# Clustered attention and a gated FFT layer on one core: engine order written by hand, dependent steps put off by a set number of places, reciprocal rows spread by two DMAs

## The chip, the cores and the metric

One core of a Trainium2 chip. The metric is the device time of one execution in microseconds (us), lower is better. The engines are PE (matmul; its weight loads are shown as PEld), DVE (vector), ACT (scalar activation), POOL (GpSimd) and SP, which here issues DMAs only. Each engine takes its own instructions in order and waits at semaphores for the others; sixteen DMA engines move data.

## The reference

The first half is attention in which a query only sees keys of its own cluster; the second half is a long convolution by FFT between two gates.

```python
B, H, S, D = 4, 8, 768, 64          # n_clusters = 16
q_assign = argmax(einsum('bhsd,hcd->bhsc', q_n, c_n))      # q_n, k_n, c_n: normalised
k_assign = argmax(einsum('bhsd,hcd->bhsc', k_n, c_n))
mask = q_assign[:, :, :, None] == k_assign[:, :, None, :]
scores = where(mask, q @ k.T / sqrt(D), -1e9)
attn = softmax(scores)
x = (attn @ v).transpose(0, 2, 1, 3).reshape(B, S, H * D)  # (4, 768, 512)
x1, x2, x3 = split(x @ w_proj, 3)                          # w_proj: 512 x 1536
x2_conv = irfft(rfft(x2, axis=1) * rfft(filter_fft, axis=0))
out = (x1 * x2_conv * x3) @ w_out                          # (4, 768, 512)
```

Inputs and output are float32 in HBM.

## The kernel before

The work runs in eight groups (`groups`): one batch and four of its eight heads. A group has two pairs of heads (`Pair`), a pair has six steps, one for each block of 128 keys. That makes 96 steps; w is the step within the group (0 to 11), sk the step within the pair (0 to 5).

**A step.** For each of the two heads, `scores` (L332) multiplies keys by queries into a PSUM tile ps (two buffers), and ACT takes the exponential into one of six SBUF tiles p (L336). The cluster mask is part of the matmul: `routing` writes the one-hot cluster of each row, times a large number, into extra rows of the operand aug. Scores of step i + 1 are issued ahead of the `values` of step i. `values` (L347) multiplies the p of both heads by v into the PSUM tile o (one buffer), and DVE adds p up over the six steps in acc (L354, from sk = 1 on; acc has one buffer). After sk = 5 ACT copies o to osb (L357, L358).

**Finish of a pair.** In step sk = 0 of the next pair `finish` (L372) runs. PE sums acc over the 128 partitions with a matrix of ones (L366), ACT copies the four rows of sums to den (L369). The reciprocals are needed spread over partitions, and that is done through DRAM: den to dd (L376), dd to dn as 128 x 12 (L378), DVE adds a small number and inverts dn (L379, L380), dn to dr (L382), and one DMA copies the two rows of dr to 64 partitions each of rb (L384; 384 KB, its source has the shape 2 x 64 x 768 with a repeated middle dimension). All four DMAs are issued by SP. DVE then scales osb by rb into x32 (L387), and `store` writes the sums and differences uT on DVE (L419, L420) and xT on POOL (L421). The last pair of all takes another way, over PE (`finish_on_pe`).

**Fill places.** Between a step's matmuls stand fills: the generators `routing` (of the next group), `hyena` (the second half of the model, for the batch before) and `tables` (in group 0). Each `yield` ends one fill. A list `fill` holds a generator, the number of fills it has left and the step by which it should be through; from these each step works out its number nf and issues half of them after the scores of the first head and half after those of the second (`emit`). One fill of PE work ends in a PSUM tile pf (two buffers) that ACT or DVE reads.

`routing` transposes q and k (L271, copies on ACT L273, casts into aug on POOL L278 and L279) and has SP load the next q and k into the buffer just read (L86); matches with the centroids (L284), transposes the result (L293), and finds the first best cluster on DVE (L295, L296, then L300, L302, L304, which give the one-hot oh). After three empty fills PE transposes oh (L310), DVE writes ohT (L312), and SP copies it to aug with eight DMAs (L316). `hyena` projects (L436), multiplies by the spectrum of the filter (`convolve`: L249 and L253 on PE, L447 on DVE, L450 on POOL), computes gates (L460, L463, L465), transforms back (`invert`: L478, a copy od on ACT L481, yy on DVE L485 and L486, y2 on POOL L487) and projects out (L499). `tables` loads the filter (L200, L201), forms its sum and difference on DVE (L217, L218) and its spectrum. `forward_tables` makes the sine tables: arithmetic on DVE (L185 to L190), the sines on ACT (L192).

**Order.** `tc.manual_schedule` is given PE alone (L529): PE's instructions keep the order in which the program issues them. Those of ACT, DVE, POOL and SP, DMA issues among them, are put in order by the scheduler of the framework before the run, by its own estimate of when operands are ready, so they may be moved ahead of instructions that the program issues earlier.

Of the kernel before, what the change touches and what calls it, by code (L numbers as in the profile page):

```python
# [13 lines left out]
F32 = mybir.dt.float32  # L14
# [3 lines left out]
Alu = mybir.AluOpType  # L18
# [12 lines left out]
def kernel(  # L31
# [11 lines left out]
    nc = tc.nc  # L43
    ctx.enter_context(nc.allow_non_contiguous_dma(reason="layouts"))
    B, H, S, D = q.shape
# [8 lines left out]
    EPS = 1e-30  # L54
# [11 lines left out]
    def bank():  # L66
        if spare:
            return spare.pop(0)
        if more_banks[0]:
            more_banks[0] += 1  # L70
            if more_banks[0] % 4 in (0, 2):
                w = psS.tile([128, 2, 512], F32, name="ps")
                spare.append(w[:, 1])
                return w[:, 0]
        return psF.tile([128, 512], F32, name="pf")[:]


    raw = ctx.enter_context(tc.tile_pool(name="raw", bufs=4))
# [28 lines left out]
    c = cen.tile([128, D], F32)  # L107
# [50 lines left out]
    at = ctx.enter_context(tc.tile_pool(name="at", bufs=1))  # L158
# [19 lines left out]
    nc.gpsimd.memset(kc[:, 0, 192:193], 384.0)  # L178
    nc.gpsimd.memset(sh[:, 0, 192:193], 192.0)

    def forward_tables():
        MAGIC = 12582912.0
        for m in range(3):
            sm = cen.tile([128, 1], F32)
            nc.vector.tensor_scalar(sm, sq, float(2 * m), None, op0=Alu.add)  # L185
            n, r = (pbuf[2 * m + i][:, :S].rearrange("p (a b) -> p a b", a=2) for i in range(2))
            nc.vector.scalar_tensor_tensor(n, kc, sm, sh, op0=Alu.mult, op1=Alu.add)
            nc.vector.tensor_scalar(r, n, 1.0 / S, MAGIC, op0=Alu.mult, op1=Alu.add)
            nc.vector.tensor_scalar(r, r, MAGIC, -float(S), op0=Alu.subtract, op1=Alu.mult)
            nc.vector.tensor_tensor(n, n, r, op=Alu.add)  # L190
            for i in range(2):
                nc.scalar.activation(fw[i][:, m], n[:, i], Act.Sin, scale=2.0 * math.pi / S)  # L192

# [66 lines left out]
    def routing(n):  # L260
        aset, g = n % NSET, n % 2
        qkT = {}
        for pr in range(2):
            for j in range(2):
                qr = qk_raws.pop((n, pr, j))
                z = 2 * pr + j
                qkT[z] = rt.tile([128, 2, 384], F32, name="qkT", bufs=4)
                for ch in range(2):
                    tps = bank()
                    for t in range(3):  # L270
                        nc.tensor.transpose(tps[:, ts(t, 128)],  # L271
                                            qr[:, 3 * ch + t].rearrange("p h d -> p (h d)"), ident)
                    nc.scalar.copy(qkT[z][:, ch], tps[:, :384])  # L273
                    if ch == 1:
                        load_qk(n + 1, pr, j)
                    yield
                qf = qkT[z][:].rearrange("p a b -> p (a b)")
                (nc.gpsimd if n else nc.vector).tensor_copy(augs[aset][0][:D, z], qf[:D])  # L278
                nc.gpsimd.tensor_copy(augs[aset][1][D:, z], qf[D:])  # L279
        sim = rt.tile([128, 2, 384], F32, name="sim")  # L280
        for ch in range(2):
            sim_ps = bank()
# [19 lines left out]
        nc.vector.tensor_reduce(m2, cf, axis=AX, op=Alu.max)  # L302
        oh = rt.tile([128, 48, NC], BF16, name="oh")
        nc.vector.tensor_tensor(oh, cf, m2[:].unsqueeze(2).to_broadcast([128, 48, NC]), op=Alu.is_equal)  # L304
        for _ in range(3):
            yield
        ohf = oh[:].rearrange("p n c -> p (n c)")
        oT = bank()[:].bitcast(BF16)
# [12 lines left out]
    class Pair:  # L321
# [17 lines left out]
        def values(self, sk):  # L339
# [13 lines left out]
                    a = pb[hp][0][:, :S] if sk == 1 else acc[hp]  # L353
                    nc.vector.tensor_tensor(acc[hp], a, pb[hp][sk][:, :S], op=Alu.add)  # L354
            if sk == NT - 1:
                self.osb = at.tile([128, S + 1], F32, name="osb", bufs=2)
                nc.scalar.copy(self.osb[:, :384], self.o[:, 0, :384])  # L357
                nc.scalar.copy(self.osb[:, 384:], self.o[:, 1, :385])  # L358

        def sums(self):  # L360

# [10 lines left out]
        def finish(self):  # L372

            den = self.sums()
            dd = dram.tile([4, 384], F32, name="dd")
            nc.sync.dma_start(dd, den[0:128:32])  # L376
            dn = at.tile([128, 12], F32, name="dn")
            nc.sync.dma_start(dn, dd[:].rearrange("z (a b) -> (z a) b", b=12))  # L378
            nc.vector.tensor_scalar(dn, dn, EPS * S, None, op0=Alu.add)  # L379
            nc.vector.reciprocal(dn, dn)  # L380
            dr = dram.tile([2, S], F32, name="dr")
            nc.sync.dma_start(dr[:].rearrange("z (a b) -> (z a) b", b=12), dn)  # L382
            rb = at.tile([128, S], F32, name="rb")
            nc.sync.dma_start(rb, dr[:].unsqueeze(1).to_broadcast([2, 64, S]))  # L384
            x32 = at.tile([128, NT, 128], F32, name="x32")
            xf = x32[:].rearrange("p t c -> p (t c)")
            nc.vector.scalar_tensor_tensor(xf, self.osb[:, :S], self.osb[:, S:S + 1], rb,  # L387
                                           op0=Alu.add, op1=Alu.mult)
            self.store(x32)

        def finish_on_pe(self):

# [31 lines left out]
    def hyena(b, xT, uT, last=False):  # L424
# [16 lines left out]
        def convolve():  # L441
            for i in range(3):
                tm = [hw.tile([128, 2, DM], F32, name="tm", bufs=3) for r in range(2)]
                for cs in range(2):
                    ps = spectrum(i, cs, uv2[:, 0], uv2[:, 1])
                    for r in range(2):
                        nc.vector.tensor_tensor(tm[r][:, cs], ps, hm[:, i, 2 * r + cs], op=Alu.mult)  # L447
                    yield
                for r in range(2):
                    (nc.vector if last and r else nc.gpsimd).tensor_tensor(  # L450
                        y[:, i, r], tm[r][:, 0], tm[r][:, 1], op=Alu.add)

        def gates(dt):
            x3 = pbuf[dt][:, :S] if last else hw.tile([128, S], F32, name="x3", bufs=2)
# [13 lines left out]
        def invert(dt):  # L468
            po, pe = bank(), bank()
            steps = [(0, 0, 0, 0, 128), (0, 1, 1, 0, 128), (2, 0, 4, 0, 64), (2, 1, 5, 0, 64)]  # L470
            for n in range(4):
# [7 lines left out]
                                     start=(n == 0), stop=(n == 3))  # L479
            od = hw.tile([128, 384], F32, name="od")  # L480
            nc.scalar.copy(od, po[:, :384])  # L481
            yy = hw.tile([128, NT, 128], F32, name="yy")
            ov = od[:].rearrange("p (t c) -> p t c", c=64)
            ev = pe[:, :384].rearrange("p (t c) -> p t c", c=64)
# [1 line left out]
            nc.vector.tensor_tensor(yy[:, :, 64:], ev, ov, op=Alu.subtract)  # L486
            (nc.vector if last and dt % 2 else nc.gpsimd).tensor_tensor(  # L487
                y2[:, dt], yy[:].rearrange("p t c -> p (t c)"), gate[dt], op=Alu.mult)
            yield
            yield  # L490

        def expand():
# [32 lines left out]
        for _ in gen:  # L525
            pass

    NR, NH, NTAB = 17, 43, 13
    ctx.enter_context(tc.manual_schedule(engines={mybir.EngineType.PE}))  # L529
    groups = [(b, g) for b in range(B) for g in range(2)]  # L530
    more_banks[0] = 1
    drain(routing(0))
    more_banks[0] = 0
    forward_tables()
    nc.gpsimd.memset(augs[1][1][:D], 0.0)
    load_v(*groups[1])
    xu = {}
# [17 lines left out]
    def emit(nf):  # L555
        for _ in range(nf):
            for f in fill:
                if f[1] > 0:
                    f[1] -= 1
                    next(f[0], None)  # L560
                    break
# [4 lines left out]
    for i, (n, pr, sk) in enumerate(steps):  # L566
# [15 lines left out]
        if w == 4 and n == 0:  # L582
            nc.gpsimd.dma_start(wpj, moe_w_proj.rearrange("(t p) m -> p t m", p=128))
            nc.gpsimd.dma_start(wout, moe_w_out.rearrange("(t p) m -> p t m", p=128))
        if w == 5 and g == 0 and n > 0:
            hq = hyena(b - 1, *xu[b - 1])
            fill.append([hq, NH // 2, 12])

        nf = 0
        for f in fill:  # L590
            nf += -(-f[1] // max(1, f[2] - w))
        scores(i + 1, 0)
        emit((nf + 1) // 2)
        scores(i + 1, 1)
        emit(nf // 2)
        if sk == 0 and i:
            pairs[steps[i - 1][:2]].finish()
        pairs[n, pr].values(sk)
    fin = pairs[steps[-1][:2]].finish_on_pe()
    for _ in range(4):  # L600
        next(fin, None)
# [34 lines left out]
```

## Time and profile before

| | us |
|---|---|
| median of 2 runs (650.2 to 653.59) | 651.89 |
| the profiled execution, its own time | 651.56 |
| its span, first to last instruction | 649.7 |
| PE busy | 455.3 (70%) |
| DVE busy | 341.5 (53%) |
| ACT busy | 259.3 (40%) |
| POOL busy | 151.4 (23%) |
| mean granted PE clock, as a share of 2.4 GHz | 0.865 |

The profile is of one execution. Busy time leaves out semaphore waits, branches and the issuing of DMAs. An instruction's idle time is put down to the one that released it last. The granted clock has two levels here, 1.0 (2.4 GHz) and 0.5 (1.2 GHz). "SPq" rows are DMA issues on SP: the time on the row is that of the issue, not of the transfer.

### The profile page before, as it was taken

The numbers are of one execution on the slowest core, as the hardware profiler recorded it, in microseconds if no ns is written. First come the engines' busy times: TensorE is split into PE (matmuls) and PEld (weight loads), VectorE is DVE, ScalarE is ACT, GpSimd is POOL, SyncE is SP. The second block draws the span as 40 slices with busy tenths as digits, with TensorE's granted clock in tenths as the row PEclk, the third lists the DMA queues.
The fourth block names the chain that finished last, engine by engine and source line by source line (L and its number), as shares of the span: only waits on it lengthen the run. The fifth ranks groups of instructions, "written<-read, shape, count | busy, mean of one in ns | idle before, by whom it ended". The sixth has DMA issues, their size and how long they took to land.

```text
span 649.7 us, 6805 instructions
## 1 busy us (share of the span) xinstructions
PE 455.3 (70%) x2426; PEld 184.8 (28%) x2426; DVE 341.5 (53%) x474; ACT 259.3 (40%) x430; POOL 151.4 (23%) x154
## 2 busy tenths in 40 slices
PE   1538899089249587779785885789667688958565
PEld 0323334034113242224222342323222233313221
DVE  0937655572836535453652835553553755832632
ACT  2434576147214262337353262436334146324021
POOL 6500514101403241222300541222300430210211
PEclk9959899689759697799999798889879699779798
DMA  9930423104300042005410041004000000002002
GB/s 255 202 74 7 96 68 90 49 14 113 72 23 11 17 113 59 13 14 168 97 30 25 1 126 47 12 24 150 22 17 21 5 2 26 1 25 97 0 1 97
DMA packets 66518, 37.05 MB, mean 57 GB/s; under 512 B 56042, under 2 KB 61734, under 8 KB 66486
## 3 DMA queue, kind: packets, MB, share of 16 engines
q1 hardware_dynamic: 61430, 32.14, 17.7%
q0 software_dynamic: 1088, 2.13, 1.7%
q10 hardware_dynamic: 3968, 2.36, 1.5%
q8 instruction: 19, 0.31, 0.2%
q14 instruction: 13, 0.11, 0.0%
HBM read 30.66 MB, written 6.48 MB: 57 GB/s over the span
## 4 chain that ended last, share of the span: by engine, by line
PE 42%; DMA 23%; DVE 19%; issue 6%; ACT 6%; POOL 1%; SPq 1%; DVEq 0%; ACTq 0%; POOLq 0%
DMA rb<-dr 19%; PE o L347 15%; PE ps L332 7%; PE pf L460 5%; PE pf L499 3%; DMA dr<-dn 2%; PE pf L366 2%; PE pf L478 2%; DVE tm L447 2%; DMA vraw<-in_v_dram 1%; PE ps L460 1%; PE pf L436 1%; POOL hy L487 1%; DVE uT L420 1%; ACT qkT L273 1%
## 5 line engine op out<-in xcount | busy, mean ns | idle before, releaser
L347 PE MATMUL o<-p_141,vraw 128*64 128x385 f32 (+1 forms) x128 | 58.1, 584 | 0.0
L347 PE MATMUL o<-p_142,vraw 128*64 128x385 f32 (+1 forms) x128 | 58.1, 584 | 0.0
L336 ACT ACTIVATE p_144<-ps 128x768 f32<-128x768 f32 x32 | 26.3, 822 | 76.7 <-PE ps L332 75.9
L460 PE MATMUL pf<-xT,wpj 128*128 128x384 bf16 x212 | 46.4, 351 | 9.8 <-DVE tm L447 6.6
L347 PE MATMUL o<-p_146,vraw 128*64 128x385 f32 (+1 forms) x128 | 52.1, 533 | 0.0
L347 PE MATMUL o<-p_145,vraw 128*64 128x385 f32 (+1 forms) x128 | 52.1, 533 | 0.0
L310 PE MATMUL pf<-identb,oh 128*128 128x128 bf16 x42 | 5.1, 283 | 64.8 <-DVE oh L304 64.8
L347 PE MATMUL o<-p_144,vraw 128*64 128x385 f32 (+1 forms) x128 | 48.9, 506 | 0.0
L347 PE MATMUL o<-p_143,vraw 128*64 128x385 f32 (+1 forms) x128 | 48.9, 505 | 0.0
L336 ACT ACTIVATE p_145<-ps 128x768 f32<-128x768 f32 x32 | 25.9, 810 | 54.9 <-PE ps L332 54.9
L336 ACT ACTIVATE p_141<-ps 128x768 f32<-128x768 f32 x32 | 25.9, 811 | 41.9 <-PE ps L332 37.1
L450 POOL TENSOR_TENSOR hy<-tm 128x512 bf16<-128x512 f32 x21 | 28.1, 1353 | 51.1 <-DVE tm L447 31.7
L336 ACT ACTIVATE p_142<-ps 128x768 f32<-128x768 f32 x32 | 26.1, 815 | 29.6 <-PE ps L332 27.4
L460 PEld LDWEIGHTS <-wpj 128*128 128x128 bf16 x256 | 26.1, 104 | 38.2 <-issue 16.6
L336 ACT ACTIVATE p_143<-ps 128x768 f32<-128x768 f32 x32 | 26.2, 819 | 24.3 <-PE ps L332 24.1
L278 POOL CAST aug_138<-qkT 64x768 bf16<-64x768 f32 x16 | 15.8, 988 | 79.4 <-ACT qkT L273 78.8
L499 PE MATMUL pf<-wout,hy 128*128 128x512 bf16 x80 | 23.8, 426 | 13.5 <-DVE yy L486 6.9
L271 PE MATMUL pf<-ident,qkraw 128*128 128x128 f32 x174 | 27.3, 284 | 7.8 <-ACT qkT L273 7.5
L332 PE MATMUL ps<-aug_136 80*128 80x384 bf16 x96 | 24.6, 339 | 6.4 <-DMA aug_136<-ohT 5.5
L336 ACT ACTIVATE p_146<-ps 128x768 f32<-128x768 f32 x32 | 26.1, 817 | 6.7 <-PE ps L332 5.4
L478 PE MATMUL pf<-inv,hy 128*128 128x384 bf16 (+1 forms) x108 | 21.5, 358 | 10.2 <-DVE ohT L312 5.1
L332 PE MATMUL ps<-aug_137 128*128 128x384 bf16 x96 | 26.3, 359 | 2.2 <-ACT p_141 L336 2.2
(509 smaller groups left out, 1006.5 us busy)
## 6 DMA issues: line engine op xcount, KB each, us to landing
qkraw<-in_q_dram SPq DMA_DIRECT2D x32, 192.0 KB
vraw<-in_v_dram SPq DMA_DIRECT2D x8, 768.0 KB
out_dram<-tm SPq DMA_DIRECT2D x12, 512.0 KB
rb<-dr SPq DMA_DIRECT2D x15, 384.0 KB
qkraw<-in_k_dram SPq DMA_DIRECT2D x28, 192.0 KB
hy<-in_moe_filter_fft_dram ACTq DMA_DIRECT2D x4, 384.0 KB
wpj<-in_moe_w_proj_dram POOLq DMA_DIRECT2D x1, 1536.0 KB, 11.7
qkraw<-in_k_dram ACTq DMA_DIRECT2D x4, 192.0 KB
```

What stands on the lines that cost most here:

```text
L271: nc.tensor.transpose(tps[:, ts(t, 128)], qr[:, 3 * ch + t].rearrange("p h d -> p (h d)"), ident)
L273: nc.scalar.copy(qkT[z][:, ch], tps[:, :384])
L278: (nc.gpsimd if n else nc.vector).tensor_copy(augs[aset][0][:D, z], qf[:D])
L332: nc.tensor.matmul(sps[:, ch, :384], self.aug[hp][:K, 2 * self.pr + 1, ts(sk, 128)], self.aug[hp][:K, 2 * self.pr, ts(ch, 384)], start=Tru ...
L336: nc.scalar.activation(p[:, :S].rearrange("p (a b) -> p a b", a=2), sps[:, :, :384], Act.Exp, scale=0.125)
L347: nc.tensor.matmul(self.o[64 * hp:64 * hp + 64, ch, :384 + ch], vv[:, 2 * self.pr + hp, sk * D:(sk + 1) * D], pb[hp][sk][:, 384 * ch:384 * ...
L366: nc.tensor.matmul(dps[32 * z:32 * z + 32, :384], ones32, self.acc[hp][:, ts(ch, 384)], start=True, stop=True)
L447: nc.vector.tensor_tensor(tm[r][:, cs], ps, hm[:, i, 2 * r + cs], op=Alu.mult)
L450: (nc.vector if last and r else nc.gpsimd).tensor_tensor(y[:, i, r], tm[r][:, 0], tm[r][:, 1], op=Alu.add)
L460: nc.tensor.matmul(ps[:, :384], wpj[:, kt, off + dt * 128:off + dt * 128 + 128], xT[:, kt, ts(ch, 384)], start=(kt == 0), stop=(kt == ND - 1))
L478: nc.tensor.matmul((pe, po)[e][:, :384], y[lo:hi, i, cs, ts(dt, 128)], inv[lo:hi, row], start=(n == 0), stop=(n == 3))
L499: nc.tensor.matmul(ps, y2[:, kt, ts(2 * tt + e, 128)], wout[:, kt], start=(kt == 0), stop=(kt == ND - 1))
```

## The change

All five engines keep the order of the program: `manual_schedule` is given ACT, DVE, POOL and SP too. So that an engine doesn't reach an instruction before its operands are there, the program issues some of them later. `later(n, fn)` puts fn on a list, and `tick()`, called twice in each step, counts down and calls what is due. With it

- the copies of o to osb come one tick after the pair's last values (`take`);
- of the finish, dn is loaded 2 ticks after the sums, inverted (with the DMA to dr) after 4, spread to rb after 6, and scaled and stored after 9;
- rb is written by two DMAs, one for each head, each from one row of dr to 64 partitions.

Other parts of the program are moved: the arithmetic of the sine tables goes between the casts of the first `routing`, the sines after it; `routing` has four empty fills instead of three before L310 (NR 18 instead of 17); POOL's additions in `convolve` are issued ahead of the yield; in `invert` one of the two yields comes between the copy od and yy; `hyena` starts at w = 6 instead of 5. What the program issues in `tables` (the loads of the filter on ACT's queue, the sum and the difference on DVE) and at w = 4 (the loads of w_proj and w_out) now stays at that place.

```diff
+    put_off = []
+    def later(n, fn):
+        put_off.append([n, fn])
+    def tick():
+        for f in put_off:
+            f[0] -= 1
+        while put_off and min(f[0] for f in put_off) <= 0:
+            f = next(f for f in put_off if f[0] <= 0)
+            put_off.remove(f)
+            f[1]()
...
-    def forward_tables():
+    def forward_tables(m):
...
-        for m in range(3):
+        if m < 3:
...
+    def forward_sines():
+        for m in range(3):
...
+                if n == 0 and z:
+                    forward_tables(z - 1)
...
-        for _ in range(3):
+        for _ in range(4):
             yield
...
             if sk == NT - 1:
-                self.osb = at.tile([128, S + 1], F32, name="osb", bufs=2)
-                nc.scalar.copy(self.osb[:, :384], self.o[:, 0, :384])
-                nc.scalar.copy(self.osb[:, 384:], self.o[:, 1, :385])
+                later(1, self.take)
...
-            nc.sync.dma_start(dn, dd[:].rearrange("z (a b) -> (z a) b", b=12))
-            nc.vector.tensor_scalar(dn, dn, EPS * S, None, op0=Alu.add)
-            nc.vector.reciprocal(dn, dn)
+            later(2, lambda: nc.sync.dma_start(dn, dd[:].rearrange("z (a b) -> (z a) b", b=12)))
             dr = dram.tile([2, S], F32, name="dr")
-            nc.sync.dma_start(dr[:].rearrange("z (a b) -> (z a) b", b=12), dn)
+            def invert():
+                nc.vector.tensor_scalar(dn, dn, EPS * S, None, op0=Alu.add)
+                nc.vector.reciprocal(dn, dn)
+                nc.sync.dma_start(dr[:].rearrange("z (a b) -> (z a) b", b=12), dn)
+            later(4, invert)
             rb = at.tile([128, S], F32, name="rb")
-            nc.sync.dma_start(rb, dr[:].unsqueeze(1).to_broadcast([2, 64, S]))
+            def spread():
+                for hp in range(2):
+                    nc.sync.dma_start(rb[64 * hp:64 * hp + 64], dr[hp:hp + 1].to_broadcast([64, S]))
+            later(6, spread)
             x32 = at.tile([128, NT, 128], F32, name="x32")
-            nc.vector.scalar_tensor_tensor(xf, self.osb[:, :S], self.osb[:, S:S + 1], rb,
-                                           op0=Alu.add, op1=Alu.mult)
-            self.store(x32)
+            def scale():
+                nc.vector.scalar_tensor_tensor(x32[:].rearrange("p t c -> p (t c)"), self.osb[:, :S],
+                                               self.osb[:, S:S + 1], rb, op0=Alu.add, op1=Alu.mult)
+                self.store(x32)
+            later(9, scale)
...
+                    for r in range(2 if cs else 0):
+                        (nc.vector if last and r else nc.gpsimd).tensor_tensor(
+                            y[:, i, r], tm[r][:, 0], tm[r][:, 1], op=Alu.add)
                     yield
-                for r in range(2):
-                    (nc.vector if last and r else nc.gpsimd).tensor_tensor(
-                        y[:, i, r], tm[r][:, 0], tm[r][:, 1], op=Alu.add)
...
             nc.scalar.copy(od, po[:, :384])
+            yield
...
-            yield
             yield
...
-    NR, NH, NTAB = 17, 43, 13
-    ctx.enter_context(tc.manual_schedule(engines={mybir.EngineType.PE}))
+    NR, NH, NTAB = 18, 43, 13
+    E = mybir.EngineType
+    ctx.enter_context(tc.manual_schedule(engines={E.PE, E.Activation, E.DVE, E.Pool, E.SP}))
...
-    forward_tables()
+    forward_sines()
...
-        if w == 5 and g == 0 and n > 0:
+        if w == 6 and g == 0 and n > 0:
...
         scores(i + 1, 0)
+        tick()
         emit((nf + 1) // 2)
         scores(i + 1, 1)
+        tick()
         emit(nf // 2)
...
+    tick()
     fin = pairs[steps[-1][:2]].finish_on_pe()
```

## Rows read from the trace of the kernel before

**Rows 1.** The page: PE's busy time, and its granted clock in 40 slices.

```profile
PE 455.3 (70%) x2426; PEld 184.8 (28%) x2426; DVE 341.5 (53%) x474; ACT 259.3 (40%) x430; POOL 151.4 (23%) x154
...
PEclk9959899689759697799999798889879699779798
```

**Rows 2.** Windows before, in and after the 96 steps: length, then busy times.

```profile
48.30:574.20 525.90, 394.33 (x2152) 156.85 (x2148) 288.31 (x382) 227.72 (x375) 120.53 (x99) 0.87 0.17 48
0.00:48.30 48.30, 15.81 (x77) 8.88 (x79) 23.06 (x43) 16.55 (x28) 19.23 (x47) 0.81 0.80 178
574.20:649.70 75.50, 45.14 (x201) 19.09 (x201) 30.13 (x49) 15.06 (x29) 11.63 (x8) 0.85 0.11 44
```

**Rows 3.** The page: the chain that ended last, by line.

```profile
DMA rb<-dr 19%; PE o L347 15%; PE ps L332 7%; PE pf L460 5%; PE pf L499 3%; DMA dr<-dn 2%; PE pf L366 2%; PE pf L478 2%; DVE tm L447 2%; DMA vraw<-in_v_dram 1%; PE ps L460 1%; PE pf L436 1%; POOL hy L487 1%; DVE uT L420 1%; ACT qkT L273 1%
```

**Rows 4.** The same chain in order of time, 112 to 150 us: start, length.

```profile
117.29 10.28 DMA rb<-dr
...
132.62 0.82 PE pf L310 x6
...
137.95 1.44 PE o L347 x8
...
140.15 1.45 PE o L347 x8
...
147.17 1.63 DMA dr<-dn
```

**Rows 5.** The tile rb: idle time of DVE before it (us, times).

```profile
  DMA rb<-dr: 107.7, 15
```

**Rows 6.** PE's waits: line, releaser: us in total, times, longest.

```profile
PE pf L310 <- DVE oh L304: 64.8, 7, 20.9
PE pf L249 <- DVE tm L447: 19.8, 3, 9.8
...
PE pf L499 <- DVE yy L486: 6.9, 1, 6.9
PE pf L460 <- DVE tm L447: 6.6, 1, 6.6
...
PE pf L478 <- DVE ohT L312: 5.1, 2, 3.3
...
PE pf L366 <- DVE acc_3554 L354: 2.6, 1, 2.6
```

**Rows 7.** Windows of two of PE's pauses, columns as in rows 2.

```profile
114.40:132.60 18.20, 0.01 (x1) 0.00 (x0) 10.77 (x16) 2.16 (x4) 1.39 (x2) 0.62 0.16 44
...
465.10:476.50 11.40, 0.00 (x0) 0.00 (x0) 4.91 (x8) 0.81 (x1) 0.82 (x1) 0.59 0.08 31
```

**Rows 8.** Windows of the 15 stretches at clock 0.5, 77.9 to 559.2: their sum.

```profile
sum 133.00, PE 69.18 PEld 23.90 DVE 68.38 ACT 14.28 POOL 22.34; mean PE 4.61 PEld 1.59 DVE 4.56 ACT 0.95 POOL 1.49
```

**Rows 9.** Windows with qkraw loads, then rb alone; last: clock, DMA share, GB/s.

```profile
173.00:174.50 1.50, 0.00 (x0) 0.00 (x0) 1.50 (x4) 0.00 (x0) 0.00 (x0) 0.50 1.09 243
175.00:182.00 7.00, 0.00 (x0) 0.00 (x0) 1.25 (x2) 0.00 (x0) 0.00 (x0) 0.50 0.13 51
```

**Rows 10.** The timeline of SP, 138 to 163 us: start, length of the issue.

```profile
139.51 0.59 SPq L316 DMA_DIRECT2D aug_137<-ohT  x1
...
148.82 0.59 SPq L384 DMA_DIRECT2D rb<-dr  x1
...
152.17 5.79 SPq L376 DMA_DIRECT2D dd<-den  x1
...
162.69 0.32 SPq L378 DMA_DIRECT2D dn<-dd  x1
```

**Rows 11.** Groups by form: an accumulation of DVE; count, busy us, mean ns.

```profile
L354 DVE TENSOR_TENSOR acc_1003<-acc_1003,p_146 128x768 f32<-128x768 f32 x2 | 1.9, 952 | 0.0
```

**Rows 12.** The timeline of DVE before the loop: the first filter sum.

```profile
25.05 1.74 DVE L217 TENSOR_TENSOR x_395<-hy 128x1536 bf16<-128x1536 f32 x1
```

**Rows 13.** DVE's waits: line, releaser: us in total, times, longest.

```profile
DVE yy L485 <- ACT od L481: 19.6, 10, 2.9
```

More of the change, by code (lines that the diff above doesn't have):

```diff
@@ L190, in forward_tables @@
             nc.vector.tensor_tensor(n, n, r, op=Alu.add)
+    def forward_sines():
+        for m in range(3):
+            n = pbuf[2 * m][:, :S].rearrange("p (a b) -> p a b", a=2)
             for i in range(2):
@@ L355, in values, with take @@
             if sk == NT - 1:
-                self.osb = at.tile([128, S + 1], F32, name="osb", bufs=2)
-                nc.scalar.copy(self.osb[:, :384], self.o[:, 0, :384])
-                nc.scalar.copy(self.osb[:, 384:], self.o[:, 1, :385])
+                later(1, self.take)
+        def take(self):
+            self.osb = at.tile([128, S + 1], F32, name="osb", bufs=2)
+            nc.scalar.copy(self.osb[:, :384], self.o[:, 0, :384])
+            nc.scalar.copy(self.osb[:, 384:], self.o[:, 1, :385])
         def sums(self):
@@ L377, in finish @@
             dn = at.tile([128, 12], F32, name="dn")
-            nc.sync.dma_start(dn, dd[:].rearrange("z (a b) -> (z a) b", b=12))
-            nc.vector.tensor_scalar(dn, dn, EPS * S, None, op0=Alu.add)
-            nc.vector.reciprocal(dn, dn)
+            later(2, lambda: nc.sync.dma_start(dn, dd[:].rearrange("z (a b) -> (z a) b", b=12)))
             dr = dram.tile([2, S], F32, name="dr")
-            nc.sync.dma_start(dr[:].rearrange("z (a b) -> (z a) b", b=12), dn)
+            def invert():
[3 more added lines that the diff above has]
+            later(4, invert)
             rb = at.tile([128, S], F32, name="rb")
-            nc.sync.dma_start(rb, dr[:].unsqueeze(1).to_broadcast([2, 64, S]))
+            def spread():
+                for hp in range(2):
+                    nc.sync.dma_start(rb[64 * hp:64 * hp + 64], dr[hp:hp + 1].to_broadcast([64, S]))
+            later(6, spread)
             x32 = at.tile([128, NT, 128], F32, name="x32")
-            xf = x32[:].rearrange("p t c -> p (t c)")
-            nc.vector.scalar_tensor_tensor(xf, self.osb[:, :S], self.osb[:, S:S + 1], rb,
-                                           op0=Alu.add, op1=Alu.mult)
-            self.store(x32)
+            def scale():
[3 more added lines that the diff above has]
+            later(9, scale)
         def finish_on_pe(self):
```

## The prediction

> **What bounds the kernel now.** I read the page's busy shares first [rows 1]. PE is the busiest engine and yet is busy only 70% of the span, and its clock line keeps dropping from 9 to 5 or 7 tenths. So the time lies in waits, and the question is where. The windows by stage [rows 2] give the weights: 48.3 us before the first values matmul, 525.9 us for the 96 steps, 75.5 us after. In the 96 steps PE is busy 394.3 us, so it stands still for 131.6.
>
> Next the page's chain by line [rows 3]: its first entry is the DMA rb<-dr, 19% of the span. The chain in order of time, near 115 us [rows 4], shows why a transfer for one pair of heads stops everything: rb takes 10.28 us, then come x (L387) and the routing's reduction and oh on DVE (L302, L304), and only then, 15.3 us after the issue, PE's L310. The scheduler has put L387 ahead of L300 to L304 on DVE, and DVE takes its instructions in order, so routing and sums that were ready stood behind the transfer. The view of rb [rows 5] has the total: DVE sat idle 107.7 us before its 15 L387. PE's own waits [rows 6] say what this cost PE. L310 waited 64.8 us for oh in 7 places. The three longest take 18.2, 20.9 and 11.4 of it (50.5; [rows 7] have the first and the third, with PE empty and rb in flight); the other 14.3 is the oh chain itself (three pauses of about 4.1 and one of 2.0). To rb also belong L249 19.8, L460 6.6, L478 5.1 and four single waits of 2.1 to 2.6 (L366 and L478, one of them shown), 9.6. Together **91.6 us of the 131.6**, and L499's 6.9 after the loop.
>
> After such pauses the granted clock is 0.5, its 1.2 GHz level. The 15 stretches at that level between 48 and 574 us last 133.0 us and hold 69.2 us of PE work [rows 8]. At 2.4 GHz this work would take half as long, so the low level costs 34.6 us.
>
> **The change part by part.** The profiled execution took 651.6 us (span 649.7), 0.3 below the median of the two runs, so I sum against 651.6.
>
> *The reciprocal rows.* While only rb runs, the DMA engines are 0.13 busy, which is two of sixteen; just before, with 192 KB qkraw loads, all sixteen are [rows 9]. The new form has two transfers of 192 KB, whose source and target both start with a dimension of 64. From below, a hop that moves 6 KB takes 1.63 us [rows 4], and with two issues of 0.59 [rows 10] that is 2.8; from above, 10.3 + 0.6. I take the nearest row, a load of the same 192 KB on all engines: 0.8 us each at the 243 GB/s of [rows 9], so 2.8 + 1.6 = 4.4 us. Of the Trainium skill one rule speaks against this part: "DMA: Bandwidth & Descriptors", section "Rules for kernel authors", says of two transfers to disjoint partition halves not to bother, since they share the same engines. By it the rows would come as late as now, which is the first rival below; no run here shows such a split yet.
>
> *The places.* The steps are followed by two ticks each. The chain begins at the end of a pair's step 0; dn is loaded at the second tick of step 1, inverted at that of step 2, spread at that of step 3, and scaled at the first tick of step 5. From spread to scale there are 1.5 steps: 3.3 us where a step is bare (2.20 us from one to the next [rows 4]), and 6.7 at the mean forecast below (430 / 96). So 4.4 us are covered nearly everywhere and DVE does not wait for rb. I take off the 91.6, and 5 of the 6.9 after the loop: **-96.6**. Cover gone, a late transfer costs DVE the difference, in the rivals below. What is late next is the oh chain and DVE itself: in a bare step two accumulations of 0.95 [rows 11] fill 1.9 of 2.2 us.
>
> *The clock.* The pauses that go are 91.6 of 131.6, 0.70 of PE's idle time. The same share of 34.6 is **-24** (ends 12 and 34.6).
>
> *The oh chain.* A fourth empty fill place goes in before L310. The four pauses left (14.3 us) shrink where the place carries other work. DVE needs about 4.2 us from mx to oh, and between lie one values and two scores (2.2): about 2 us of each 4.1 stays. **-6** (ends 0 and -12).
>
> *Ahead of the loop.* The two filter sums (L217, L218, 1.74 us the first and 1.75 the second [rows 12]) and four filter loads leave the preamble, where the sums stand on the chain; the table arithmetic goes between the routing casts instead. 3.5 us of sums and some load time: **-5** (ends -9 and +3). They come back inside the first two steps: the loads are issued on ACT only when tables() begins, and the seventh fill place wants the sums some 6 to 8 us later. **+6** (ends 0 and 12).
>
> *The fixed order on DVE, ACT, POOL and SP.* No work is added, but an instruction can no longer be overtaken. Worst is SP: the eight copies of ohT are issued 0.6 us apart (5 us), and qkraw loads at the start of a group have held an issue for 5.79 us [rows 10]; the chain's four DMAs stand behind them, and DVE's inversion, behind which the accumulations queue, stands behind those. From below it costs nothing (the places are late enough); from above 5.8 us for each of 15 pairs, 87. The nearest row is the 5 us of ohT copies, which 7 pairs meet; half of it is covered by the step's own length: 7 x 2.5 = 17.5, and a little for the rest: **+20**.
>
> *At nothing:* copying o a tick later (two copies on ACT, which is busy 227.7 of 525.9 us [rows 2]; a microsecond for each of 15 pairs if they do come late), POOL's y additions issued ahead of the yield, the yield between od and yy (DVE's wait for od, 19.6 us in all [rows 13], is no wait of PE), and the gate stage beginning at step 6 (its matmuls move, none is added).
>
> **The sum:** 651.6 - 96.6 - 24 - 6 - 5 + 6 + 20 = **546 us**, 16% less. The loop alone: 525.9 - 91.6 - 24 - 6 + 6 + 20 = 430 us, in which PE is busy 394 - 24 = 370 (86%) and DVE 288 (67%), so neither shares nor work forbid it.
>
> **Rivals.**
> *The rows stay slow.* Each half is still moved by two engines or fewer, 10.3 us in all. Then DVE waits 10.3 - 6.7 = 3.6 us at the scale, 54 us over 15 pairs where it was 107.7; PE lost 98.5 us for those 107.7, so 49 come back, and 9 of clock: 604 us. For it: nothing in this trace shows a transfer of this form. Against: the two busy engines match the leading 2 of the old source, and 64 rows of 3 KB are no longer led by a 2. The Trainium skill, same page, section on why a DMA adds 16 to its semaphore, has a rule on this side: the largest count up to 16 that divides both slowest dimensions, which is 2 before and 16 after; the trace agrees for before.
> *The order by hand takes back most of it.* Each pair costs its 5.8 us: 546 - 20 + 87 = 613 us. For it: dd to dn took 10.5 us at 152 us [rows 10] instead of 1.7. Against: what filled the queue there was rb on its two engines together with the loads.
> *Slower: SP's order.* Every hop of the chain (dd, dn, dr, rb) stands on SP behind qkraw loads and ohT copies, and DVE behind each hop. If every hop takes the 10.5 us seen once, the chain is 42 us against 4.5 steps x 4.5 = 20 us of room: DVE waits 22 us in each of the 7 pairs that meet loads, 154 us, and 546 + 154 = 700 us. It ends above today's 652 from 106 us of such waits on, which is a hop of 9 us (4 x 9 - 20 = 16 us, times 7). Against: three of the four hops move 6 KB, and a hop that met no loads took 1.63.
>
> **How the numbers follow.** Forecast 0.68; rows stay slow 0.10; order by hand 0.13; SP's order 0.09, of which 0.05 is slower and 0.04 falls short of that threshold and lands within 2%. Two per cent is 13 us, about what a measurement of this kernel tells from no change. So faster 0.91, same 0.04, slower 0.05. The forecast's own range is 499 (no new waits, all of the clock back, the other terms at their lower ends: 546 - 20 - 10.6 - 6 - 4 - 6) to 584 (twice the new waits, half of the clock, the filter loads at 12: 546 + 20 + 12 + 6). To hold 8 in 10 it must reach to the slow rows: 499 to 604.
>
> **What would show it.** Right: the wait of L387 for rb under 20 us in all; L384 twice per pair and rb landing within about 5 us; no PE pause over 6 us in the loop; L310's wait for oh under 12 us; PE busy over 80% in the loop, at 0.93 of the clock or more. L379, the inversion, would be the first place of a new wait; after it PE's L366 behind the last accumulations. Wrong: rb still at 10 us, or DVE idle before L379 by more than 80 us in all, or SP issues of 5 us as a rule, or a first step over 15 us for the filter sums.

## The result, and the profile after

The changed kernel takes 582.31 us (median of 2 runs, 581.71 to 582.91) against 651.89: a ratio of 0.893, 95% interval 0.883 to 0.904. The forecast was 546 us, in a range of 499 to 604. The direction and the main cause hold; the gain is 70 us where 106 were forecast.

The page of the kernel after: busy times, PE's granted clock, the chain that ended last by line, and the issue group of rb (lines are those of the changed kernel).

```profile
PE 443.7 (76%) x2426; PEld 183.1 (32%) x2426; DVE 353.2 (61%) x474; ACT 260.3 (45%) x430; POOL 145.3 (25%) x154
...
PEclk9856989889799898999979998999989999999798
...
PE o L367 12%; PE ps L352 6%; SPq L336 5%; DVE tm L482 4%; PE pf L389 4%; DMA rb<-dr 4%; PE pf L471 3%; PE pf L534 3%; PE pf L495 3%; DVE uT L455 2%; PE pf L304 2%; PE pf L289 2%; DVE cand L316 2%; PE ps L495 2%; ACT qkT L291 2%
...
rb<-dr SPq DMA_DIRECT2D x30, 192.0 KB, 3.3
```

PE's share rises from 70% to 76% [rows 1], with 12 us less of it (455.3 to 443.7): the same number of matmuls at a better granted clock. On the chain the rows' transfer falls from 19% to 4% [rows 3]. A new entry stands third: L336, the copies of ohT, which are issues on SP. Each half of rb lands 3.3 us after its issue; the one transfer took 10.28 [rows 4].

The windows before, in and after the 96 steps, columns as in [rows 2], and rb alone in flight, which answers to [rows 9].

```profile
0.00:47.10 47.10, 15.86 (x79) 8.89 (x81) 21.86 (x40) 16.80 (x28) 16.25 (x45) 0.76 0.47 118
47.10:510.00 462.90, 382.69 (x2152) 155.38 (x2148) 303.32 (x390) 228.46 (x375) 118.68 (x102) 0.94 0.24 61
510.00:580.60 70.60, 45.18 (x205) 18.82 (x201) 28.02 (x45) 15.03 (x28) 10.41 (x7) 0.90 0.11 45
...
426.80:430.00 3.20, 0.00 (x0) 0.00 (x0) 0.00 (x0) 0.55 (x1) 0.00 (x0) 1.00 0.40 123
```

The loop went from 525.9 to 462.9 us: PE's busy time fell by 11.6 (394.3 to 382.7), its idle time by 51.4 (131.6 to 80.2). With rb in flight the DMA engines are 0.40 busy and move 123 GB/s, where the old form had 0.13 and 51: more than two of the sixteen now take part.

The waits of PE and DVE (line, releaser: us, times, longest), and the tile rb.

```profile
PE pf L330 <- DVE oh L324: 11.4, 5, 2.3
...
PE pf L389 <- DVE acc_3092 L374: 8.3, 1, 8.3
PE pf L389 <- DVE acc_2123 L374: 6.5, 1, 6.5
...
PE pf L389 <- DVE acc_793 L374: 4.1, 1, 4.1
...
PE pf L267 <- DVE x_395 L235: 3.7, 1, 3.7
```

```profile
DVE dn L405 <- DMA dn<-dd: 31.9, 6, 7.3
```

```profile
  DMA rb<-dr: 14.0, 6
...
DMA to landing us min/median/max: 3.1/3.3/3.4
```

DVE's wait for rb is 14.0 us in 6 places instead of 107.7 in 15 [rows 5], and PE's wait for oh 11.4 us, none over 2.3 [rows 6]. What is new is L405, the inversion, 31.9 us, and after it PE's L389, the sums, behind the last accumulations: 25.3 us in seven places (2.2, 2.0, 1.6 and 0.6 besides those shown), where the kernel before had 6.1 in three (2.6, 2.6 and 0.9; [rows 6] show the first). The longest of these pauses is seen best in the timelines of SP, DVE and PE (start, length, line; in brackets the idle time before it and its releaser).

```profile
420.51 0.57 SPq L336 DMA_DIRECT2D aug_138<-ohT  x1
...
424.92 0.59 SPq L336 DMA_DIRECT2D aug_139<-ohT  x1
425.55 1.23 SPq L414 DMA_DIRECT2D rb<-dr  x2
```

```profile
423.00 0.95 DVE L374 TENSOR_TENSOR acc_3093<-acc_3093,p_144 128x768 f32<-128x768 f32 x1
430.02 1.02 DVE L420 SCALAR_TENSOR_TENSOR x_3090<-osb,rb 128x768 f32<-128x768 f32 x1 [6.07 <-DMA rb<-dr]
...
432.65 0.94 DVE L374 TENSOR_TENSOR acc_3092<-acc_3092,p_145 128x768 f32<-128x768 f32 x1
433.51 0.95 DVE L374 TENSOR_TENSOR acc_3093<-acc_3093,p_146 128x768 f32<-128x768 f32 x1
```

```profile
433.65 1.49 PE L389 MATMUL pf<-acc_3092,ones_96 128*32 128x384 f32 x4 [8.28 <-DVE acc_3092 L374]
```

Eight copies of ohT hold SP for 5 us, so rb is issued late. On DVE the scaling and its stores stand ahead of the pair's last accumulations, whose operands are ready, and PE's sums stand behind those. In four of the seven groups that have such copies (3 to 6, counted from 0) they stand right ahead of rb like this; in the first three they stand ahead of dd.

### The profile page after: what moved, and what is told of

It reads as the page before. It is cut to its first block, busy times and chain, and to the rows that moved or that the text cites. A ratio compares the mean times of both kernels' runs of the same rounds, so it can differ in the third digit from the quotient of the medians.

```text
span 580.6 us, 6780 instructions
## 1 busy us (share of the span) xinstructions
PE 443.7 (76%) x2426; PEld 183.1 (32%) x2426; DVE 353.2 (61%) x474; ACT 260.3 (45%) x430; POOL 145.3 (25%) x154
## 3 DMA queue, kind: packets, MB, share of 16 engines
q1 hardware_dynamic: 61880, 32.14, 20.1%
## 4 chain that ended last, share of the span: by engine, by line
PE 39%; DVE 32%; DMA 8%; ACT 6%; SPq 6%; issue 5%; POOL 2%; ACTq 0%; DVEq 0%; POOLq 0%
PE o L367 12%; PE ps L352 6%; SPq L336 5%; DVE tm L482 4%; PE pf L389 4%; DMA rb<-dr 4%; PE pf L471 3%; PE pf L534 3%; PE pf L495 3%; DVE uT L455 2%; PE pf L304 2%; PE pf L289 2%; DVE cand L316 2%; PE ps L495 2%; ACT qkT L291 2%
## 5 line engine op out<-in xcount | busy, mean ns | idle before, releaser
L367 PE MATMUL o<-p_141,vraw 128*64 128x385 f32 (+1 forms) x128 | 55.8, 565 | 0.0
L367 PE MATMUL o<-p_142,vraw 128*64 128x385 f32 (+1 forms) x128 | 55.8, 565 | 0.0
L367 PE MATMUL o<-p_143,vraw 128*64 128x385 f32 (+1 forms) x128 | 48.5, 502 | 0.0
L367 PE MATMUL o<-p_144,vraw 128*64 128x385 f32 (+1 forms) x128 | 48.5, 502 | 0.0
L367 PE MATMUL o<-p_145,vraw 128*64 128x385 f32 (+1 forms) x128 | 48.2, 499 | 0.0
L367 PE MATMUL o<-p_146,vraw 128*64 128x385 f32 (+1 forms) x128 | 48.2, 499 | 0.0
L495 PE MATMUL pf<-xT,wpj 128*128 128x384 bf16 x212 | 43.1, 333 | 5.0 <-ACT od L516 1.5
L482 DVE TENSOR_TENSOR tm<-pf,hm 128x512 f32<-128x512 f32 x40 | 25.0, 680 | 20.7 <-PE pf L267 19.9
L289 PE MATMUL pf<-ident,qkraw 128*128 128x128 f32 x174 | 28.1, 289 | 11.4 <-ACT qkT L291 9.8
L495 PEld LDWEIGHTS <-wpj 128*128 128x128 bf16 x256 | 24.9, 99 | 32.9 <-issue 16.2
L291 ACT COPY qkT<-pf 128x384 f32<-128x384 f32 x58 | 26.3, 493 | 5.7 <-PE pf L289 5.1
L367 PEld LDWEIGHTS o<-p_141,vraw 128*64 128x64 f32 x128 | 17.0, 154 | 32.0 <-issue 30.5
L289 PEld LDWEIGHTS pf<-ident,qkraw 128*128 128x128 f32 x174 | 21.2, 146 | 18.3 <-ACT qkT L291 13.9
```

What stands on the lines that cost most here:

```text
L289: nc.tensor.transpose(tps[:, ts(t, 128)], qr[:, 3 * ch + t].rearrange("p h d -> p (h d)"), ident)
L367: nc.tensor.matmul(self.o[64 * hp:64 * hp + 64, ch, :384 + ch], vv[:, 2 * self.pr + hp, sk * D:(sk + 1) * D], pb[hp][sk][:, 384 * ch:384 * ...
L495: nc.tensor.matmul(ps[:, :384], wpj[:, kt, off + dt * 128:off + dt * 128 + 128], xT[:, kt, ts(ch, 384)], start=(kt == 0), stop=(kt == ND - 1))
```

## The experiments

Theory A: the gain is the transfer's form; the order by hand costs time, and the put-offs only keep that cost bearable. Rival B: the gain comes from the order and the places, and the form matters little. Each run is compared with the kernel before on the same chip; e1 to e4 share one set of runs of it. Line numbers are those of each run's own kernel: the scaling, L420 in the change, is L387 before, L388 in e2 and L424 in e9.

**One transfer again, all else as after** (e1).

```diff
-                for hp in range(2):
-                    nc.sync.dma_start(rb[64 * hp:64 * hp + 64], dr[hp:hp + 1].to_broadcast([64, S]))
+                nc.sync.dma_start(rb, dr[:].unsqueeze(1).to_broadcast([2, 64, S]))
```

> The changed kernel with the reciprocal rows spread by one DMA of shape 2 x 64 x 768 as before, all else kept (order by hand, put-off places). Theory A (the transfer is the cause, and the put-off places cover only some 3 to 7 us of it): rb again takes about 10 us, DVE waits for it 4 to 7 us in most of the 15 pairs (60 to 100 us in all, against 14.0 now), and the time is 615 to 650 us. Theory B (the order and the places are the cause, the form of the DMA matters little): DVE's wait stays under 35 us and the time under 600.

644.66 us, 0.990 of before (0.985 to 0.994). The tile rb and PE's wait for the accumulations:

```profile
  DMA rb<-dr: 78.5, 12
```

```profile
PE pf L389 <- DVE acc L374: 62.8, 7, 14.2
```

Without the new form nearly all of the gain is gone: +62 us. DVE waits for rb 78.5 us instead of 14.0, and PE waits 62.8 us at L389, where the change has 25.3.

**Two transfers alone, all else as before** (e2).

```diff
-            nc.sync.dma_start(rb, dr[:].unsqueeze(1).to_broadcast([2, 64, S]))
+            for hp in range(2):
+                nc.sync.dma_start(rb[64 * hp:64 * hp + 64], dr[hp:hp + 1].to_broadcast([64, S]))
```

> The kernel before, with the one edit that rb is written by two DMAs of 64 rows; PE alone in hand-written order, nothing put off. Theory A: rb lands in about 3.3 us, DVE's wait for it falls from 107.7 to 10 to 30 us, and most of PE's pauses go: 555 to 590 us, that is as good as the whole change. Theory B: the scheduler still puts the scaling ahead of routing and sums, the hops ahead of rb are waited for instead, and the time is above 615 us.

559.60 us, 0.858 (0.853 to 0.862): these two lines alone beat the whole change by 23 us. The loop's window, PE's waits for oh, for the filter's products and for the gates, and from PE's timeline three of the places at oh and one at L249:

```profile
48.90:492.90 444.00, 379.30 (x2143) 153.72 (x2151) 295.35 (x387) 227.56 (x376) 127.45 (x101) 0.95 0.22 57
```

```profile
PE pf L310 <- DVE oh L304: 27.1, 7, 5.1
PE pf L249 <- DVE tm L448: 8.5, 5, 3.2
...
PE pf L479 <- DVE x L466: 3.0, 3, 2.5
```

```profile
117.93 0.82 PE L310 MATMUL pf<-identb,oh 128*128 128x128 bf16 x6 [2.94 <-DVE oh L304]
158.80 0.82 PE L310 MATMUL pf<-identb,oh 128*128 128x128 bf16 x6 [5.14 <-DVE oh L304]
...
308.49 1.44 PE L249 MATMUL pf<-hy,fw 128*128 128x512 bf16 x3 [3.23 <-DVE tm L448]
...
407.77 0.82 PE L310 MATMUL pf<-identb,oh 128*128 128x128 bf16 x6 [4.74 <-DVE oh L304]
```

No scaling on DVE waits for rb in this run (10 to 30 us were expected). Yet PE is still idle for 64.7 us of the loop (444.0 - 379.3): all seven oh pauses are still there. The four that had nothing to do with rb are as long as they were (2.0 and three of 4.1). The three that were 18.2, 20.9 and 11.4 us long are 2.94, 5.14 and 4.74. Of the two long ones at L249 (9.4 and 9.8 of the 19.8 us of [rows 6]) 3.23 us each are left.

**No put-offs** (e3).

```diff
     def later(n, fn):
-        put_off.append([n, fn])
+        fn()
```

> The changed kernel with every put-off operation issued at once at its old place in the program (take, the load of dn, the inversion, the spread, the scaling), all five engines still in hand-written order and rb by two DMAs. Theory A: DVE then stands at the inversion for dd and dn (3.5 us) and at the scaling for dr and rb (5 us), with nothing allowed past it: 8 to 10 us in each of 15 pairs, 120 to 150 us, and the time is 670 to 720 us, slower than the kernel before. Theory B (with the short transfer the places are not needed): under 610 us.

709.85 us, 1.090 (1.086 to 1.094): 58 us slower than before, with the fast transfer in place. DVE's waits:

```profile
DVE dn L405 <- DMA dn<-dd: 122.7, 15, 12.8
DVE x L420 <- DMA rb<-dr: 87.2, 15, 8.1
```

In the order by hand DVE stands through the whole chain in each of the 15 pairs, 14.0 us a pair, where 8 to 10 were expected. The put-offs are worth 127 us, but only because that order is there.

**The order by hand for PE alone, all else as after** (e4).

```diff
-    ctx.enter_context(tc.manual_schedule(engines={E.PE, E.Activation, E.DVE, E.Pool, E.SP}))
+    ctx.enter_context(tc.manual_schedule(engines={E.PE}))
```

> The changed kernel with PE alone in hand-written order: the scheduler orders ACT, DVE, POOL and SP again, while the places in the program, the two DMAs and the moved yields stay. Theory A (the transfer is nearly all): 565 to 590 us, within 2% of the change, with the filter loads hoisted to the start again and the first step shorter. Theory B (the hand-written order of the four other engines is what pays): above 610 us.

552.36 us, 0.847 (0.843 to 0.851): 30 us faster than the change as it stands, 7 faster than the two transfers alone, and below the range expected. Its loop, PE's wait for oh, and a stretch of SP and of DVE with eight ohT copies:

```profile
49.70:484.10 434.40, 374.31 (x2145) 154.01 (x2151) 291.56 (x387) 228.87 (x376) 125.02 (x101) 0.95 0.22 58
```

```profile
PE pf L330 <- DVE oh L324: 22.3, 7, 4.3
```

```profile
116.93 5.87 SPq L336 DMA_DIRECT2D aug<-ohT  x8
122.90 0.53 SPq L399 DMA_DIRECT2D dd<-den  x1
```

```profile
127.80 0.96 DVE L374 TENSOR_TENSOR acc<-acc,p 128x768 f32<-128x768 f32 x1 [0.31 <-ACT p L356]
128.68 0.17 DVE L405 TENSOR_SCALAR dn<-dn 128x12 f32<-128x12 f32 x1
128.75 0.95 DVE L374 TENSOR_TENSOR acc<-acc,p 128x768 f32<-128x768 f32 x1
```

The scheduler puts the same eight copies ahead of the chain on SP and loses nothing by it, because it puts the inversion on DVE where dn is there. So SP's order alone isn't what costs; a late chain together with a fixed place on DVE is. Against e4 the change has 28.5 us more in the loop: 8.4 of PE's busy time (the clock is 0.94 against 0.95, and the trace of e4 lacks some matmuls) and 20.1 of idle time.

**Which place costs what.** Four kernels mend one place each in the changed kernel: the ohT copies issued on POOL from the second group on (e5), the chain's three steps two places later (e6), the filter's loads and sums before the loop (e7), a fifth empty fill before the transpose of oh (e8).

```diff
-                nc.sync.dma_start(augs[aset][hp][64 - 16 * hp:80 - 16 * hp, z], ohT[r0:r0 + 16])
+                (nc.sync if n == 0 else nc.gpsimd).dma_start(augs[aset][hp][64 - 16 * hp:80 - 16 * hp, z], ohT[r0:r0 + 16])
```

> The changed kernel with the eight copies of ohT issued by POOL instead of SP (from group 1 on), all else kept. Theory P (what the hand-written order costs is mostly SP: the copies stand 5 us ahead of dd or rb on its queue, and DVE waits behind them): DVE's wait before the inversion falls from 31.9 to under 10 us, the one for rb from 14.0 to under 4, the PE pauses of 6.5 and 8.3 us ahead of the sums go, and the time is 555 to 566 us. Theory Q (DVE is simply full there, the scaling standing ahead of the last accumulations): the waits go but the pauses stay at 2 to 4 us each, and the time is 570 to 580.

564.98 us, the median of 556.05, 564.63, 565.33 and 565.60, which lie too far apart for an interval. DVE's wait for dn:

```profile
DVE dn L405 <- DMA dn<-dd: 22.7, 6, 5.8
```

About 17 us come back by the median and 26 by the fastest execution. DVE still stops before the inversion in six places, 22.7 us where under 10 were expected: its place is too early even with SP free.

```diff
-            later(4, invert)
+            later(6, invert)
...
-            later(6, spread)
+            later(8, spread)
...
-            later(9, scale)
+            later(11, scale)
```

> The changed kernel with later places: inversion at 6 ticks instead of 4, spread at 8 instead of 6, scaling at 11 instead of 9, which is behind the last accumulations; SP's order kept. Theory P: both of DVE's waits fall below 8 us together although the copies stay on SP, and with the scaling out of the way of the accumulations the pauses ahead of the sums in steps 5 and 11 of groups 0, 1, 4 and 6 fall under 2 us each: 548 to 560 us. Theory Q's other side (DVE has no room, work put later only moves the pause): 570 us or more.

573.70 us, 0.881 (0.875 to 0.887), 9 less than the change; the intervals of the two ratios overlap. The loop, and PE's wait at the projection:

```profile
46.90:492.90 446.00, 376.13 (x2155) 153.44 (x2151) 300.16 (x388) 227.80 (x376) 121.15 (x102) 0.97 0.25 63
```

```profile
PE pf L471 <- DVE uT L454: 7.0, 3, 3.8
```

DVE's wait for dn falls to 7.0 us, but that for rb stays at 11.9, since SP's order is kept. L389's waits for the accumulations fall by 23 us, to 2.1, yet PE's idle time in the loop only by 10.3 (80.2 to 69.9): the rest came back in other places, the largest part of it at the projection behind uT, 7.0 us where the change has 1.8.

```diff
+    filt = []
...
     def forward_sines():
...
-    def tables():
...
         flo = hy.tile([128, 3, DM], F32, name="hy")
...
+        nc.vector.tensor_tensor(fd, flo, fhi, op=Alu.subtract)
+        filt.extend((fu, fd))
...
-        nc.vector.tensor_tensor(fd, flo, fhi, op=Alu.subtract)
+        fu, fd = filt
```

> The changed kernel with the four filter loads issued on ACT's queue ahead of the sines, and the filter's sum and difference on DVE right behind the first routing, all else kept. If the 19.1 us that DVE waits for the filter cost PE what its first two steps are longer than with the scheduler's order (18.5 us here, 11.7 in the run that leaves four engines to the scheduler), the time is 573 to 577 us. If the preamble becomes longer by the same work, it stays at 580 to 584.

577.50 us, 0.887 (0.882 to 0.893). The first step, from its values to the next step's, takes 6.65 us instead of 11.70. The time falls by 4.8, and the intervals of the two ratios overlap: it can't be told from no change.

```diff
-        for _ in range(4):
+        for _ in range(5):
             yield
...
-    NR, NH, NTAB = 18, 43, 13
+    NR, NH, NTAB = 19, 43, 13
```

> The changed kernel with a fifth empty fill place ahead of the transposes of oh (NR 19). If the four pauses of 2.3 us (groups 3 to 6, step 2) are only a place too early, they go and nothing else moves: 572 to 577 us. If what follows (copies of ohT on SP, the spread behind them) comes later by as much, the pauses ahead of the sums grow instead and the time is 580 to 590.

573.21 us, 0.880 (0.875 to 0.886): 9 less, with intervals that overlap a little, and not for the reason given. The pauses at oh only went from 2.3 to 2.0 us each; the gain lies in the longest two at L389, from 6.5 and 8.3 to 2.8 and 1.1. SP's timeline at the place of the pause of 8.3 us, and the tile rb, show how:

```profile
418.36 1.11 SPq L414 DMA_DIRECT2D rb<-dr  x2
419.56 4.97 SPq L336 DMA_DIRECT2D aug<-ohT  x8
```

```profile
  DMA rb<-dr: 0.9, 4
```

The extra fill moves the transposes of oh, and with them the eight copies, behind rb. So it is in all four groups in which they stood ahead of it, and DVE's wait for rb falls from 14.0 to 0.9 us. e5 and e8 thus mend in part the same thing.

**All four mended** (e9): e5, e7 and e8 together, with the places at 5, 7 and 10.

> The changed kernel, all five engines still in hand-written order, with what the single runs pointed to put together: copies of ohT on POOL, the filter early, a fifth empty place, and the inversion, the spread and the scaling one tick later (5, 7, 10). If the cost of the hand-written order is these four places and no more, the savings add: 582 - 17 - 5 - 9 = 551 us or a little less, level with the run in which the scheduler orders four engines (552). If something else in the fixed order costs as much, it stays above 562 us.

565.22 us, 0.866 (0.861 to 0.871). PE's wait that is left:

```profile
PE pf L393 <- DVE acc L378: 14.3, 6, 4.4
```

14 us above the 551 that the single gains would add up to. They could not simply be added, since e5 and e8 overlap; and the wait that is left is as large as what is missing: the scaling still stands ahead of the last accumulations.

**The scaling behind them** (e12): e9 with one number changed.

```diff
-            later(10, scale)
+            later(11, scale)
```

> The mended hand order once more with one place changed: the scaling comes 11 places after the sums instead of 10, which puts it behind the last accumulations of the pair; the inversion stays at 5 and the spread at 7. In the run before, the sums on PE (L393) still waited 14.3 us in 6 places for accumulations that stood behind the scaling and the stores. If the scaling's place is what is left of the cost of the hand order, these 14.3 us go and the time falls from 565 to between 548 and 556, with no other wait of PE grown by more than 3 us. If the pause only moves, as it did when all three places were put back, the waits for uT at the projection (L475) and for the one-hot rows take at least half of it over, and the time stays between 560 and 568.

552.79 us, 0.850 (0.844 to 0.856), 12 us less than e9. The loop, and the wait at the projection:

```profile
45.60:473.10 427.50, 369.44 (x2155) 152.36 (x2151) 296.01 (x388) 227.57 (x376) 146.64 (x158) 0.98 0.26 64
```

```profile
PE pf L475 <- DVE uT L458: 3.5, 1, 3.5
```

L393's wait for the accumulations is down to 2.2 us, and the projection's grew by only 1.7 (1.8 in e9). The window is that of the fastest of five executions (548.07). With the four mends and this place the order by hand is as fast as the scheduler's with none (e4).

**The scheduler with two of the mends** (e10): e4 with e5 and e8.

> The run with PE alone in hand-written order (552 us) and in it the copies of ohT on POOL and the fifth empty place. If the pauses of 3.7 to 4.3 us ahead of the transposes of oh, which that run still has in groups 3 to 6, shrink as they did in the hand-written order, 540 to 548 us; if the scheduler already works around both, 550 to 554.

538.87 us, 0.822 (0.816 to 0.828): the fastest of all, 43 us below the change, with a loop of 421.4 us. PE's waits for oh are down from 22.3 to 16.4 us; what each of the two mends gave was not run apart.

**Two DMAs, or the leading dimension?** (e11, the kernel before with this edit)

```diff
-            nc.sync.dma_start(rb, dr[:].unsqueeze(1).to_broadcast([2, 64, S]))
+            nc.sync.dma_start(rb, dr[0:1].to_broadcast([128, S]))
```

> The kernel before with rb written by ONE DMA of the same 384 KB whose leading dimension is 128: all 128 partitions get the first of the two rows of reciprocals (the second head of a pair is scaled by the first head's, so that part of the computation is left out). If the leading dimension of 2 was the cause, rb lands in 3 to 4.5 us and the time is 552 to 565 us, as with two DMAs. If it takes two DMAs, rb takes about 10 us and the time is 630 to 655.

571.23 us, 0.874 (0.867 to 0.881). The page's issue group of rb:

```profile
rb<-dr SPq DMA_DIRECT2D x15, 384.0 KB, 3.4
```

One DMA of all 384 KB lands in 3.4 us, so it isn't the number of transfers but the leading 128 (or 64) in place of the 2. The Trainium skill, "DMA: Bandwidth & Descriptors", section on why a DMA adds 16 to its semaphore, says that the count of engines is the largest up to 16 that divides both slowest dimensions; the three forms agree: 10.28 us for 2, 3.3 for 64, 3.4 for 128. The same page's advice against two transfers to disjoint halves, in "Rules for kernel authors", agrees with e11 so far as the landing goes: one transfer is as fast once its leading dimension is large. That advice speaks of halves that both run on all sixteen DMA engines; the old form, at a DMA share of 0.13, did not. Here the halves have different sources, and the split is what gives each a leading 64. The time came out 6 us above the range expected, with 10.6 us of waits of DVE for rb that e2 does not have. DVE's timeline shows where:

```profile
115.85 1.02 DVE L387 SCALAR_TENSOR_TENSOR x<-osb,rb 128x768 f32<-128x768 f32 x1 [0.88 <-DMA rb<-dr]
116.78 0.55 DVE L300 TENSOR_TENSOR cand<-cand,revc 128x768 bf16<-128x768 bf16 x1
```

In two groups the scheduler put the scaling ahead of L300 again, where e2 has it behind L304, and these two pauses at oh are 6.1 and 8.3 us long instead of 2.9 and 5.1.

## Why the prediction was right, and where it was off

**The transfer: right in kind.** It was the form, as forecast. Each half landed 3.3 us after its issue, and from the first issue to the scaling that waited for both it was 4.47 us (425.55 to 430.02), where 4.4 were taken. "The rows stay slow" is out. Of the signs named, DVE's wait for rb (14.0 us, under 20), PE's wait for oh (11.4, under 12), PE's share of the loop (83%) and its clock (0.94) came true; "no PE pause over 6 us in the loop" did not: there are two, 6.5 and 8.3.

**The step that was off** is the sum "together 91.6 us of the 131.6", and with it "the three longest take 18.2, 20.9 and 11.4 of it (50.5)", put down to rb whole. The run with the two transfers alone tests it: PE's idle time in the loop fell by 66.9 us (131.6 to 64.7), not 91.6. Of the 24.7 missing, 12.8 are what the three long pauses kept (2.94 + 5.14 + 4.74), 8.5 what L249 kept, and about 2 of the 3.0 at L479 behind the gates, the L478 of before. The last 1 or so may be the nine matmuls that the trace of e2 lacks, whose time counts as idle (an estimate: nine at the loop's mean of 0.18 us, 379.3 / 2143, are 1.6). Under the wait for rb lay a pause of the oh chain, and it stayed when rb went. The oh chain was named as "late next", but counted only at the four pauses where it showed.

**The clock: short with it.** -24 was forecast. PE's busy time in the loop fell by 15.0 us in e2, at a granted 0.95 (nine matmuls are missing there), and by 11.6 in the change as it stands, at 0.94. The size can be reached: in e12's profiled execution, at 0.98, the same matmuls take 369.4 us, 24.9 below before. What isn't shown is the step that gave it, a clock that follows PE's idle time in proportion: e6 has more idle time in its loop than e2 (69.9 us against 64.7) and a better clock (0.97 against 0.95). What holds the change at 0.94 stays open.

So rb and clock were forecast at -120.6 together and gave -92.3.

**Fixed order and filter: right in place, near in size.** +20 and +6 were forecast; e4 against the change says +30.0 for both. The first new wait is L379's (now L405), after it the sums behind the last accumulations, as named; the working "half of it is covered" was for the copies on SP, and e5 says 17 us for them by its median, against 17.5; that the two agree so well is luck, with e5's executions 10 us apart. What the prediction named as a place but gave no price is the second half: the last accumulations, which stand behind the scaling, 12 us by e12 against e9 in the mended order. The filter's first pause is 3.7 us of PE and some 5 us of the step (e7), against +6.

**The oh chain.** -6 forecast. From e2 to e4, where only the moved parts differ, the time falls by 7.2 us and oh's waits by 4.8 (27.1 to 22.3). In the order by hand they are 11.4, less than in the scheduler's.

**Ahead of the loop.** -5 forecast, -1.2 measured (48.3 to 47.1).

**The sum by the runs:** -92.3 for the transfers, -7.2 for the moved parts, +30.0 for the order by hand: -69.5 of the 69.6 measured. These are steps from one kernel to the next (before, e2, e4, the change), so they add up by construction; what they tell is the size of each. Of the rivals, "the order by hand takes back most" would have 613 us; it took back a third of the transfers' gain. "SP's order" is not what happened either: dn landed 1.5 us after its issue, dr 1.6 and rb 3.3, and DVE stood 31.9 us before the inversion, not over 80. Only without the put-offs (e3) does DVE stand through every chain.

## What to carry to other kernels

A DMA that spreads few rows over many partitions should not have the few rows as its leading dimension: look at the DMA share while it alone is in flight, and split or reshape it. Before a long wait is counted as a gain, ask what else was late at that instruction: where a shorter wait lay under the long one, only the difference comes back. And an engine order written by hand needs each place fitted to the chain's real length; one that is too early stops all that stands behind it, and one that is mended shows the next, so hand over only the engines whose order you know better.

## What was not expected of the hardware

The number of transfers hardly counted: two of 192 KB in flight together landed in 3.3 us, one of 384 KB in 3.4. Nor did size count in proportion: in the changed kernel 6 KB (dn) took 1.5 us to land, 192 KB (rb) 3.3 and 768 KB (vraw) 4.4. And the places of the order by hand seem to cost clock as well: PE's same matmuls in the loop took 382.7 us at a granted 0.94 in the change, and 369.4 at 0.98 in e12's fastest execution, in the same kind of order with its places mended.
